# Linear attention and a balanced expert layer on one core: the attention half written out in an order set by a list scheduler, with k split on GpSimd

## The chip, the cores and the metric

The kernel runs on one core of a Trainium2 chip. A core has a matrix engine (TensorE, PE in the profile), VectorE (DVE), ScalarE (ACT), GpSimd (POOL) and a queue engine (SyncE, SP), which run their own instruction lists in order and wait for each other through semaphores. 16 DMA engines move data; SyncE issues to one DMA queue (q1) and GpSimd to another (q0). The metric is device time in microseconds (us).

## The reference

Two layers, one after the other. The first is linear attention with decay, for 4 batches x 8 heads x 768 positions x 64, in blocks of 64:

```
intra = (q_b k_b^T * Dmask) v_b            # Dmask = lam^(i-j) for i >= j
inter = (q_b * lam^(i+1)) kv_state
out_b = intra + inter
kv_state = lam^64 * kv_state + (k_b * lam^(63-i))^T v_b
```

Its output, 3072 tokens of 512, is x. The second layer gives each token to one of 8 experts: all 3072 x 8 logits `x @ w_gate` are walked from the largest down, a token goes to the expert of its first entry that still has room, and an expert has room for 384 tokens. Then each expert computes `relu(x w1) w2` on its tokens. Inputs and the output are float32.

## The kernel before

The attention is done in 24 chunks of 128 tokens and all 8 heads (6 chunks a batch). For one chunk, with names and lines of `before.py`:

- **loads**: q, k and v, 256 KB each, from SyncE (`load`, L949 to L953), buffers for four chunks (`aio`, bufs=4);
- **prep** (L956 on): k is rounded to fp16 on ScalarE (L960), and what is left of it is taken on VectorE (L961), both into a tile `kp` that interleaves the halves; v is scaled on GpSimd (`vs`, L963), rounded on ScalarE (`vh`, L966), and the remainder taken on GpSimd (`vl`, L968);
- **turns**: q and k are transposed on TensorE, and copied out by ScalarE and VectorE (`qh`, `ql`, `kT`);
- **scores** (L1005): three products a head into `S`; rounded on ScalarE (L1010), remainder on VectorE (L1011), masked on GpSimd (two `affine_select` a chunk, L1014, "masks" below);
- **inter, intra** (L1033, L1045) add up in `XL`; VectorE scales that into `xs` (L1050), SyncE stores it to `x_dram` (L1078);
- **state** (L1064): k^T v is added up in PSUM and read out as `sth`, `stl`;
- **gate**: x is transposed, split (`xh`, `xl` L1087), multiplied by `w_gate`, and the logits are copied out (L1103).

Chunks are numbered 0 to 23 below; "masks of chunk 20" are its two L1014 instructions. Each GpSimd, VectorE or ScalarE instruction named here works on 128 partitions x 512 elements.

`run` writes the stages of neighbouring chunks into a loop, and the Tile framework's own scheduler puts the instructions in order. Constants for the router (`constants`, among them an `iota` of 128 x 3072 on GpSimd, L42) are written in the loop's third step, and so are the first steps of the routing (`ranges`, `ranks`: largest logits, their ranks as threshold indicators `ind1`) near its end. Seven of the sixteen expert weight loads (`load_w`, L558, 1 MB each as they land in bf16, issued by GpSimd) are tied to logits of late chunks by a one-element copy (L557); two more (`range(7, 9)`) are tied to nothing, and the scheduler issued them early.

After the last logits the routing goes on by itself: counts on TensorE against indicators, `settle` on VectorE (L215, "the first settle"), further rounds, and then the first gather of tokens (L576) for the experts. From there on the experts run; the other seven weight loads, the gathers and the scatters of results (L626) all go through GpSimd's queue.

Of the kernel before, what the change touches and what calls it, by code (L numbers as in the profile page):

```python
# [23 lines left out]
class _Router:  # L24
# [11 lines left out]
    def constants(self):  # L36
        nc, rc, P = self.nc, self.rc, 128
        V, G = nc.vector, nc.gpsimd

        def iota(name, shape, pattern, base, mult=0, dt=BF16):  # L40
            a = rc.tile(shape, dt, name=name)
            G.iota(a, pattern=pattern, base=base, channel_multiplier=mult,  # L42
                   allow_small_or_imprecise_dtypes=True)
            return a

        self.i_kt = iota("i_kt", [P, P, 24], [[1, P], [0, 24]], 1)
        self.i_j = iota("i_j", [P, 29, 24], [[1, 29], [0, 24]], 0)
        self.i_t = iota("i_t", [P, 24, 24], [[0, 24], [128, 24]], 0)
        self.i_p = iota("i_p", [P, 1], [[0, 1]], 0, 1, F32)
        self.i_e = iota("i_e", [P, 8], [[1, 8]], 0, 0, F32)  # L50
        self.i_e1 = iota("i_e1", [P, 8], [[1, 8]], 1, 0, F32)
        self.i_et = iota("i_et", [P, 24, 8], [[0, 24], [1, 8]], -8)
        self.i_g8 = iota("i_g8", [P, 9, 24], [[1, 9], [0, 24]], -8)
        self.gbase = iota("gbase", [1, 9, 24], [[384, 9], [0, 24]], 1, 0, F32)
        i_k = self.i_kt[:, :, 0]
        kvec = []
        for m, sc in enumerate((16384, 128, 1, 4096)):
            kx = rc.tile([P, P], BF16, name=f"kvec{m}")
            V.tensor_scalar(kx, i_k, float(sc), None, OP.mult)
            kvec.append(kx)  # L60
        self.kvec = kvec
        ones = {}
        for sc in (16384, 128, 64, 1):
            o = rc.tile([P, P], BF16, name=f"ones{sc}")
            V.memset(o, float(sc))
            ones[sc] = o
        self.ones = ones
        ones3 = rc.tile([3, P], F32, name="ones3")
        V.memset(ones3, 1.0)
        self.ones3 = ones3  # L70
# [5 lines left out]
        sltm = rc.tile([P, P], BF16, name="sltm")  # L76
        V.tensor_scalar(sltm, slt, 1.0, None, OP.subtract)
        self.sltm = sltm
# [3 lines left out]
        self.rmask = rmask  # L82
        rmask5 = rc.tile([P, 8, 5], F32, name="rmask5")
# [13 lines left out]
        self.ind2 = rc.tile([P, P, 24], BF16, name="ind2")  # L97
        G.memset(self.ind2[:, 64:128, :], 0.0)

    def ranges(self, L, n, ps, tag, part):  # L100
# [3 lines left out]
        if part == 0:  # L104
            self.v0 = v0 = rc.tile([P, n], F32, name="v0")
            V.reduce_max(v0, L[:, 0:n, :], axis=AX.X)
            self.mn = mn = rc.tile([P, 2], F32, name="mn")
            V.tensor_reduce(mn[:, 1:2], L[:, 0:n, :].rearrange("p t e -> p (t e)"), axis=AX.X,
                            op=OP.min)
            self.mm = mm = rc.tile([P, 3], F32, name="mm")  # L110
            V.reduce_max(mm[:, 0:1], v0, axis=AX.X)
            V.tensor_reduce(mn[:, 0:1], v0, axis=AX.X, op=OP.min)
            V.tensor_scalar(mm[:, 1:3], mn, -1.0, None, OP.mult)
            return
        if part == 1:
# [618 lines left out]
def _exact_path(ctx, tc, L, router, moe, dram):  # L734
# [398 lines left out]
def kernel(  # L1133
# [12 lines left out]
    P = 128  # L1146
# [63 lines left out]
```

## Time and profile before

| | us |
|---|---|
| median of three runs | 319.54 (315.22 to 323.77) |
| the profiled execution | 321.75 |
| its span, first to last instruction | 320.0 |
| last logits copied (L1103) | 167.90 |
| first settle (L215) | 171.06 |
| first gather issued (L576) | 189.37 |

The span falls into the attention, to 168 us, the routing, to 189 us and in part to 206 us, and the experts. A row of the timeline gives the start and the length of an instruction; `x2` means two merged into one row.

### The profile page before, as it was taken

What the parts mean: (1) busy time and instruction counts of PE and PEld (TensorE: products, weight loads), DVE (VectorE), ACT (ScalarE), POOL (GpSimd) and SP (SyncE); (2) the same over time, 40 slices, a digit from 0 to 9 for tenths busy, and PEclk for the clock granted to TensorE, in tenths of its full rate; (3) what the DMA queues carried; (4) which work ended last, traced back from release to release, by engine and by line L of the source; (5) the groups of instructions that cost most, each with busy time, mean ns of one, the idle gap of its engine ahead of it and who ended that gap; (6) DMA issues with size and microseconds to landing.
All of it is one profiled execution on the core that took longest, in us unless ns stands there. A gap on an engine that the chain in (4) does not pass through costs nothing.

```text
span 320.0 us, 8964 instructions
## 1 busy us (share of the span) xinstructions
PE 257.0 (80%) x3621; PEld 202.1 (63%) x3621; DVE 187.2 (58%) x595; ACT 166.7 (52%) x297; POOL 163.5 (51%) x189
## 2 busy tenths in 40 slices
PE   1795979979898898883759987999766999899980
PEld 0674868867777787772647676666444666577750
DVE  4558688968987788746975654577717671000000
ACT  3757687878887788625220000454242455566650
POOL 5987466674757566733436024864254226435221
PEclk9999799999999999985767785799979999999997
DMA  8999999978989899999799308999999216244211
GB/s 144 218 178 201 242 228 241 203 169 193 201 187 198 183 200 190 198 205 203 134 180 222 59 5 108 162 188 204 238 228 256 97 58 107 99 96 103 73 69 38
DMA packets 96977, 52.05 MB, mean 163 GB/s; under 512 B 76961, under 2 KB 88225, under 8 KB 96929
## 3 DMA queue, kind: packets, MB, share of 16 engines
q0 software_dynamic: 17920, 26.22, 44.2%
q1 hardware_dynamic: 79008, 25.19, 36.9%
q8 instruction: 30, 0.49, 0.6%
q14 instruction: 19, 0.15, 0.1%
HBM read 58.74 MB, written 12.58 MB: 223 GB/s over the span
## 4 chain that ended last, share of the span: by engine, by line
PE 28%; DVE 21%; DMA 19%; issue 12%; ACT 9%; POOL 8%; SPq 0%; POOLq 0%; DVEq 0%; ACTq 0%
DMA out_dram<-oe,perm 11%; DMA kf<-in_k_dram 7%; PE p L607 5%; PE p L620 5%; DVE sp L1011 5%; DVE xs L1050 4%; ACT sp L1010 3%; PE XL L1101 3%; PE spare L193 3%; DVE ql L994 3%; PE S L1005 2%; DVE xl L1087 2%; DMA xe<-x_dram,perm 2%; POOL vs L963 2%; POOL sp L1014 2%
## 5 line engine op out<-in xcount | busy, mean ns | idle before, releaser
L607 PE MATMUL p<-xeT,w 128*128 128x256 bf16 (+1 forms) x512 | 50.2, 253 | 8.5 <-ACT hT L612 4.2
L607 PEld LDWEIGHTS <-w 128*128 128x128 bf16 x512 | 40.6, 100 | 17.1 <-issue 9.9
L1014 POOL TENSOR_SCALAR_AFFINE_SELECT sp<-sp 128x512 f32<-128x512 f32 x48 | 31.4, 663 | 33.7 <-DVE sp L1011 31.2
L626 POOL DMA_INDIRECT out_dram<-oe,perm x24 | 24.2, 1007 | 43.2 <-ACT oe L625 34.0
L620 PE MATMUL p<-w,hT 128*128 128x512 bf16 x192 | 45.8, 378 | 0.0
L576 POOL DMA_INDIRECT xe<-x_dram,perm x24 | 25.3, 1053 | 36.4 <-DVE B L306 15.0
L1010 ACT CAST sp<-S 128x512 bf16<-128x512 f32 x48 | 32.4, 743 | 19.1 <-PE S L1005 19.0
L612 ACT ACTIVATE hT<-p 128x512 bf16<-128x512 f32 (+1 forms) x64 | 31.0, 493 | 18.7 <-PE p L607 12.1
L1011 DVE TENSOR_TENSOR sp<-S,sp 128x512 bf16<-128x512 f32 x48 | 32.9, 732 | 6.5 <-ACT sp L1010 6.4
L963 POOL TENSOR_TENSOR vs<-vf,lamneg 128x512 f32<-128x512 f32 x24 | 27.3, 1139 | 9.9 <-DMA vf<-in_v_dram 6.2
L625 ACT COPY oe<-p 128x512 f32<-128x512 f32 x24 | 14.0, 587 | 34.2 <-PE p L620 20.4
L594 ACT COPY xeT<-pt 128x1024 bf16<-128x1024 bf16 (+1 forms) x16 | 12.8, 800 | 35.8 <-PE pt L590 34.2
L968 POOL TENSOR_TENSOR vl<-vs,vh 128x512 bf16<-128x512 f32 x24 | 28.4, 1183 | 5.7 <-ACT vh L966 5.4
L1005 PE MATMUL S<-qh,kT 64*128 64x128 f16 x384 | 28.8, 229 | 1.3 <-DVE sp L1011 1.3
L1045 PE MATMUL XL<-vh,sp 128*128 128x64 bf16 x384 | 25.7, 202 | 4.8 <-POOL sp L1014 4.2
L620 PEld LDWEIGHTS <-hT 128*128 128x128 bf16 x192 | 17.1, 97 | 17.8 <-issue 1.4
L1045 PEld LDWEIGHTS <-sp 128*128 128x128 bf16 x576 | 22.5, 104 | 8.4 <-POOL sp L1014 7.4
L977 PE MATMUL kT_ps<-identf,kp 128*128 128x128 f32 x96 | 17.6, 313 | 10.4 <-DVE mb L126 6.0
L961 DVE TENSOR_TENSOR kp<-kf,kp 128x512 f16<-128x512 f32 x24 | 20.0, 835 | 8.3 <-ACT kp L960 8.2
L960 ACT CAST kp<-kf 128x512 f16<-128x512 f32 x24 | 18.9, 789 | 10.8 <-DMA kf<-in_k_dram 10.8
L1005 PEld LDWEIGHTS <-kT 64*128 64x128 f16 x576 | 19.7, 99 | 6.5 <-issue 3.8
L1045 PE MATMUL XL<-vl,sp 128*128 128x64 bf16 x192 | 23.1, 201 | 0.0
(259 smaller groups left out, 584.8 us busy)
## 6 DMA issues: line engine op xcount, KB each, us to landing
w<-in_moe_w_dram POOLq DMA_DIRECT2D x16, 1024.0 KB
qf<-in_q_dram SPq DMA_DIRECT2D x24, 256.0 KB, 4.7
kf<-in_k_dram SPq DMA_DIRECT2D x24, 256.0 KB, 5.2
vf<-in_v_dram SPq DMA_DIRECT2D x24, 256.0 KB, 5.3
x_dram<-xs SPq DMA_DIRECT2D x24, 256.0 KB, 3.8
xe<-x_dram,perm POOLq DMA_INDIRECT x24
out_dram<-oe,perm POOLq DMA_INDIRECT x24
lam_sb<-in_lam_dram SPq DMA_DIRECT2D x1, 4.0 KB, 2.5
```

Of the source, the lines that this page charges most:

```text
L576: nc.gpsimd.indirect_dma_start(out=xe[:, c, :], out_offset=None, in_=self.x_dram, in_offset=bass.IndirectOffsetOnAxis(ap=pm, axis=0), boun ...
L607: nc.tensor.matmul(p1[:, f, 0:n, :], self.w1t[e][:, kc, fc * P : (fc + 1) * P], j["xeT"][:, kc, 0:n, :], start=(kc == 0), stop=(kc == 3), ...
L612: nc.scalar.activation(hT[:, fp, :, 0:n, :], p1[:, :, 0:n, :], ACT.Relu)
L620: nc.tensor.matmul(p2, j["hT"][:, kc // 2, kc % 2, c, :], self.w2t[e][:, kc, :], start=(kc == 0), stop=(kc == 7))
L626: ins = nc.gpsimd.indirect_dma_start(out=self.out, out_offset=bass.IndirectOffsetOnAxis(ap=j["perms"][c], axis=0), in_=oe, in_offset=None, ...
L963: nc.gpsimd.tensor_tensor(vs, vf, self.lamneg[:, t, :, None].to_broadcast([P, 8, 64]), OP.mult)
L968: nc.gpsimd.tensor_tensor(vl, vs, vh, OP.subtract)
L1005: nc.tensor.matmul(S[a][:, hp, :], kT[r, hp, :, ks], qq[r, hp, :], start=(i == 0), stop=(i == 2))
L1010: nc.scalar.copy(s[:, :, :, 1], S[a])
L1011: nc.vector.tensor_tensor(s[:, :, :, 0], S[a], s[:, :, :, 1], OP.subtract)
L1014: nc.gpsimd.affine_select(out=sf, in_=sf, compare_op=OP.is_ge, fill=0.0, base=0, pattern=[[0, 4], [1, P]], channel_multiplier=-1)
L1045: nc.tensor.matmul(X[a][:, hp, :], sp[a][:, hp, :, ss], vv[:, h, :], start=(first and hp == 0 and i == 0), stop=(i == 2), skip_group_check ...
```

## The change

The attention is rewritten as small functions, one for each instruction group, and `OPS` lists them with the engine, an assumed duration and what each waits for (`ldk` of chunk g after `state` and `Tk` of chunk g-7, and so on). `_Plan.emit` is a list scheduler: it runs these through assumed engine times, takes the ready operation of lowest `OFF[name] + g * 4.6` on each engine, and so writes the program order of all five engines, which the framework then keeps (`manual_schedule`). In the parts:

- **k**: no fp16 rounding on ScalarE and no `kp` tile. The upper 16 bits of each float32 are read as bf16 in place; the rest is taken by one subtraction into the lower 16 bits, in place, on GpSimd (`kp0`, L1099). The planner's table gives `kp0` of even chunks to VectorE and of odd ones to GpSimd; the function always issues it on GpSimd.
- **loads** go up to six chunks ahead (k: seven buffers), and `xs` has seven buffers.
- **PSUM**: the transposes of q, k and x have a bank each (`QT`, `KT`, `XT`); the logits are added up in the bank of `XT`.
- **router**: its constants are spread over the chunks (`pool_constants`, `dve_constants`), the large `iota` in four pieces; `ranges` and `ranks` yield after each instruction, and are planned as operations of their own.
- **weights**: nine loads (`lw`) are planned on GpSimd, the first after the last load of v, each after the one before and after masks of chunks 15 to 23.

The routing after its first steps, the experts and the order of their loads are as before.

```diff
-        kp = self.wk.tile([P, 8, 64, 2], F16, tag="kp", bufs=4)
-        nc.scalar.copy(kp[:, :, :, 1], kf)
-        nc.vector.tensor_tensor(kp[:, :, :, 0], kf, kp[:, :, :, 1], OP.subtract)
...
+    def kp0(self, g):
+        kf = self.kpair(self.d[g])
+        lo = kf.bitcast(F16).rearrange("p (c j s) -> p c j s", c=4, s=2)[:, :, :, 0]
+        self.nc.gpsimd.tensor_tensor(lo, kf.rearrange("p (c j) -> p c j", c=4), self.ksplit(kf)[0],
+                                     OP.subtract)
...
+    def ksplit(self, f):
+        hi = f.bitcast(BF16).rearrange("p (c j s) -> p c j s", c=4, s=2)[:, :, :, 1]
+        lo = f.bitcast(F16).rearrange("p (c j s) -> p c j s", c=4, s=2)[:, :, :, 0]
+        return hi, lo
...
-        self.io = ctx.enter_context(tc.tile_pool(name="aio", bufs=4))
+        self.io = ctx.enter_context(tc.tile_pool(name="aio", bufs=6))
...
+    OPS = (
+        ("ldq", "SP", 1.10, None, "Tq-6"),
+        ("ldk", "SP", 1.10, None, "state-7 Tk-7"),
...
+        ("kp0", None, 0.78, None, "ldk"),
...
+        ("mk1", "Pool", 0.66, None, "spl1"),
...
+                if name == "kp0" and eng is None:
+                    eng, dur = (("DVE", 0.78), ("Pool", 1.17))[g % 2]
...
+                    m = min(max(free[e], est[i]) for i in a)
+                    i = min((ops[i][6], i) for i in a if max(free[e], est[i]) <= m + 0.05)[1]
...
-            if s == 2:
-                router.constants()
-            if 19 <= s <= 21:
-                router.ranges(logits, 18, attn.pt, "T", s - 19)
-            if s == 22:
-                router.ranks(logits, 0, 10)
...
-            if 18 <= s <= 24:
-                moe.load_w(s - 18, logits[0:1, s - 2, 0:1])
...
+        for m in range(9):
+            plan.op("lw", m, "Pool", 0.9, lambda m=m: moe.load_w(m),
+                    [("ldv", 23), ("mk1", min(15 + m, 23)), ("lw", m - 1)], 0, 4.6)
...
-    for m in range(7, 9):
-        moe.load_w(m)
```

How it moves instructions is shown at two places. The first is GpSimd around the weight loads. In its list of before, the first weight load that is tied to logits (`w_0_78`) stands ahead of the masks of chunk 18 (`sp_2955` and `sp_2959`):

```order
L968 TENSOR_TENSOR vl<-vs,vh 128x512
L558 DMA w_0_78<-in_moe_w_dram 128x4x1024
L1014 AFFINE_SELECT sp_2955<-sp_2955 128x512
L1014 AFFINE_SELECT sp_2959<-sp_2959 128x512
L963 TENSOR_TENSOR vs<-vf,lamneg 128x512
L1014 AFFINE_SELECT sp_3088<-sp_3088 128x512
L968 TENSOR_TENSOR vl<-vs,vh 128x512
L1014 AFFINE_SELECT sp_3092<-sp_3092 128x512
```

The changed list around its first weight load (`kf<-kf` is `kp0`; L1113 is `vs`, L1124 `vl`, L1184 a mask; `sp_2809` and `sp_2840` are the masks of chunk 18, the `kf` row ahead of the load is `kp0` of chunk 22):

```order
L1113 TENSOR_TENSOR vs<-vf,lamneg 128x512
L1124 TENSOR_TENSOR vl<-vs,vh 128x512
L1184 AFFINE_SELECT sp_2705<-sp_2705 128x512
L1099 TENSOR_TENSOR kf<-kf 128x512
L638 DMA w_0_70<-in_moe_w_dram 128x4x1024
L1184 AFFINE_SELECT sp_2809<-sp_2809 128x512
L1184 AFFINE_SELECT sp_2840<-sp_2840 128x512
L1124 TENSOR_TENSOR vl<-vs,vh 128x512
L1113 TENSOR_TENSOR vs<-vf,lamneg 128x512
L1184 AFFINE_SELECT sp_2942<-sp_2942 128x512
L1099 TENSOR_TENSOR kf<-kf 128x512
L1113 TENSOR_TENSOR vs<-vf,lamneg 128x512
```

The first weight load now stands behind `kp0` of chunk 22 with only one more `kp0` and two more `vs` to come, and each chunk has one GpSimd instruction more, `kp0`, which runs four to five chunks ahead of the masks. Up to the second mask of chunk 20 the changed list holds, from the second mask of chunk 0 on, 21 `kp0`, 22 `vs`, 22 `vl`, 40 masks, `identb`, the four pieces of the large `iota` and two weight loads.

The second place is VectorE around the last logits. Before, the copy of the last logits (`logits<-Lo`) is followed by six rows of `ranks` for the last 128 tokens, and then by the first settle (`S<-cps`):

```order
L156 TENSOR_TENSOR ind_607<-q_3814,i_kt 128x128x3
L168 TENSOR_SCALAR r_q_603<-y_3819 128x3
L1103 COPY logits<-Lo 128x8
L143 TENSOR_REDUCE r_v<-logits 128x1
L145 TENSOR_SCALAR y_3906<-r_v,lo,sc 128x1
L146 TENSOR_SCALAR y_3906<-y_3906 128x1
L147 TENSOR_SCALAR r_zv<-y_3906 128x1
L149 TENSOR_SCALAR ind_608<-kvec_568,r_zv 128x128
L150 TENSOR_TENSOR r_ohb<-logits,r_v 128x8
L215 TENSOR_SCALAR S<-cps 128x8
```

In the changed list the last logits' copy (the L1247 row) stands in the midst of `ranks` of the first ten chunks:

```order
L1235 TENSOR_TENSOR xl<-XT,xh 128x512
L231 TENSOR_TENSOR r_ohb<-logits,r_v 128x80
L241 TENSOR_SCALAR y_3748<-r_zv 128x10
L243 TENSOR_SCALAR r_q_3524<-y_3748 128x10
L1247 COPY logits<-XT 128x8
L246 TENSOR_TENSOR ae_3752<-r_ohb,i_et 128x80
L207 TENSOR_REDUCE r_v<-logits 128x1
L248 TENSOR_REDUCE r_am_3526<-ae_3752 128x10
L207 TENSOR_REDUCE r_v<-logits 128x10
```

From the last `xs` to that copy there are 22 rows, and from the copy to the first settle 32 more, among them `ranks` of chunks 10 to 19 and of 20 to 22 whole.

## Rows read from the trace of the kernel before

**Rows 1.** The page: its first line.

```profile
span 320.0 us, 8964 instructions
```

**Rows 2.** Windows: stretch, length, busy us of each engine (instructions), granted clock, DMA, GB/s.

```profile
43.00:120.00 77.00, 66.64 (x1417) 57.82 (x1418) 63.81 (x113) 60.74 (x110) 48.51 (x56) 1.00 0.90 200
147.00:170.00 23.00, 15.05 (x257) 12.76 (x258) 19.88 (x68) 7.94 (x14) 10.83 (x14) 0.65 0.93 171
206.00:247.00 41.00, 32.88 (x293) 21.86 (x291) 26.45 (x156) 16.31 (x26) 19.50 (x20) 0.96 1.15 217
```

**Rows 3.** Groups of instructions, 43 to 120 us: busy us, mean ns, idle before.

```profile
L1014 POOL TENSOR_SCALAR_AFFINE_SELECT sp<-sp 128x512 f32<-128x512 f32 x28 | 18.0, 651 | 26.7 <-DVE sp L1011 26.7
L968 POOL TENSOR_TENSOR vl<-vs,vh 128x512 bf16<-128x512 f32 x14 | 16.3, 1164 | 1.0 <-ACT vh L966 0.7
L963 POOL TENSOR_TENSOR vs<-vf,lamneg 128x512 f32<-128x512 f32 x14 | 15.5, 1107 | 1.2 <-DMA vf<-in_v_dram 1.2
L960 ACT CAST kp<-kf 128x512 f16<-128x512 f32 x15 | 11.9, 796 | 0.0
L961 DVE TENSOR_TENSOR kp<-kf,kp 128x512 f16<-128x512 f32 x14 | 11.5, 818 | 0.0
```

**Rows 4.** The chain of waits, whole span: start us, length us, what.

```profile
2.25 4.07 DMA kf<-in_k_dram
...
129.28 16.78 DMA kf<-in_k_dram
...
228.64 17.41 DMA out_dram<-oe,perm
```

**Rows 5.** Timeline of GpSimd: start us, length us, instruction, idle before.

```profile
1.82 3.33 POOL L42 IOTA i_kt<- 128x3072 bf16 x1
...
17.86 1.23 POOL L1014 TENSOR_SCALAR_AFFINE_SELECT sp<-sp 128x512 f32<-128x512 f32 x2
...
21.71 0.84 POOL L558 DMA_DIRECT2D w<-in_moe_w_dram  x1
...
67.68 1.48 POOL L963 TENSOR_TENSOR vs<-vf,lamneg 128x512 f32<-128x512 f32 x1
...
122.12 0.81 POOL L558 DMA_DIRECT2D w<-in_moe_w_dram  x1 [1.74 <-DVE w L557]
...
135.61 1.22 POOL L1014 TENSOR_SCALAR_AFFINE_SELECT sp<-sp 128x512 f32<-128x512 f32 x2
...
161.59 1.23 POOL L1014 TENSOR_SCALAR_AFFINE_SELECT sp<-sp 128x512 f32<-128x512 f32 x2 [2.40 <-DVE sp L1011]
...
189.37 1.59 POOL L576 DMA_INDIRECT xe<-x_dram,perm  x1 [15.02 <-DVE B L306]
```

**Rows 6.** DMA queues, 110 to 150 us: packets, MB, share of 16 engines.

```profile
q1 hardware_dynamic: 13469, 4.72, 51.0%
q0 software_dynamic: 2123, 3.17, 49.1%
```

**Rows 7.** Timeline of VectorE.

```profile
163.74 0.69 DVE L1050 TENSOR_TENSOR xs<-XL,lampow 128x512 f32<-128x512 f32 x1 [1.05 <-PE XL L1045]
...
167.90 0.22 DVE L1103 COPY logits<-Lo 128x8 f32<-128x8 f32 x1
...
171.06 0.17 DVE L215 TENSOR_SCALAR S<-cps 128x8 bf16<-128x8 f32 x1 [1.52 <-PE cps L241]
```

**Rows 8.** Groups of VectorE's instructions, 147 to 170 us.

```profile
L1011 DVE TENSOR_TENSOR sp<-S,sp 128x512 bf16<-128x512 f32 x6 | 4.1, 718 | 0.3 <-ACT sp L1010 0.3
L1087 DVE TENSOR_TENSOR xl<-xT_ps,xh 128x512 bf16<-128x512 f32 x4 | 2.7, 684 | 0.2
L156 DVE TENSOR_TENSOR ind<-q,i_kt 128x1280 bf16<-128x1280 bf16 (+1 forms) x3 | 2.4, 800 | 0.0
L1050 DVE TENSOR_TENSOR xs<-XL,lampow 128x512 f32<-128x512 f32 x3 | 2.1, 688 | 1.3 <-PE XL L1045 1.3
...
L1103 DVE COPY logits<-XL 128x8 f32<-128x8 f32 x3 | 0.5, 159 | 0.5 <-PE XL L1101 0.5
```

More of the change, by code (lines that the diff above doesn't have):

```diff
@@ L238, in first @@
             nc.tensor.matmul(cps, self.ind1[:, :, t], ohb[:, t, :], start=(t == 0), stop=False)
-        self.ranks(L, 23, 24)
+        for _ in self.ranks(L, 23, 24):
+            pass
         self.warm(0.6)
@@ L242, in first @@
         _, nm1 = settle(cps, self.ones[64])
-        self.more(23, 24)
+        for _ in self.more(23, 24):
+            pass
         z2 = sp.tile([P, 24], BF16, name="z2")
@@ new lines, in intra @@
+    def intra(self, g, a):
+        d = self.d[g]
+        first = g % 6 == 0
+        if "XL" not in d:
+            d["XL"] = self.p1.tile([128, 2, 8, 64], F32, tag="X", name="XL")
+        for hp in range(4):
+            for i, (ss, vv) in enumerate(((1, d["vh"]), (1, d["vl"]), (0, d["vh"]))):
+                self.nc.tensor.matmul(d["XL"][:, a, hp, :], d["sp"][a][:, hp, :, ss],
+                                      vv[:, 2 * hp + a, :],
+                                      start=(first and hp == 0 and i == 0), stop=(i == 2),
+                                      skip_group_check=True)
@@ L1052, in intra, with store, turn_x, xh @@
         d["xs"] = xs
[L1054 to L1057 removed]
+    def store(self, g):
+        self.nc.sync.dma_start(out=self.x_dram[g * 128 : (g + 1) * 128, :],
+                               in_=self.d[g]["xs"].rearrange("p c a d -> p (c a d)"))
+    def turn_x(self, g):
+        d = self.d[g]
+        d["xT_ps"] = self.turn(lambda hp: d["xs"][:, hp].rearrange("p a d -> p (a d)"), "XT")
+    def xh(self, g):
+        d = self.d[g]
+        d["xh"] = self.wk.tile([128, 4, 128], BF16, tag="xh", name="xh")
+        self.nc.scalar.copy(d["xh"], d["xT_ps"])
@@ new lines, in xl, with gate @@
+    def xl(self, g):
+        d = self.d[g]
+        d["xl"] = self.wk.tile([128, 4, 128], BF16, tag="xl", name="xl")
+        self.nc.vector.tensor_tensor(d["xl"], d["xT_ps"], d["xh"], OP.subtract)
+    def gate(self, g):
+        d = self.d[g]
+        d["Lp"] = Lp = d["xT_ps"][:, 0, 0:8]
+        for hp in range(4):
+            for i, (xx, ww) in enumerate(((d["xh"], self.wgh), (d["xh"], self.wgl),
+                                          (d["xl"], self.wgh))):
+                self.nc.tensor.matmul(Lp, xx[:, hp, :], ww[:, hp, :], start=(hp == 0 and i == 0),
+                                      stop=(hp == 3 and i == 2), skip_group_check=True)
```

511 lines of the change are left out of this document (306 added, 205 removed), and 24 rows, old and new, of the table OPS.

## The prediction

> **What bounds the kernel now.** I read the windows first, then the groups of instructions in the steady stretch, then the chain of waits, then the timelines of GpSimd and VectorE. The profiled span is 320.0 us [rows 1]; the run around it took 321.75, 1.75 more, and lies 0.7% above the median of the runs shown, 319.54.
>
> The steady stretch, 43 to 120 us, holds 14 chunks (14 `vs`), 5.50 us each [rows 2, 3]. TensorE is busy 66.64 us there (4.76 a chunk, 87%), VectorE 63.81 (83%), ScalarE 60.74 (79%), GpSimd 48.51 (63%), and the DMA engines 0.90 [rows 2]. No engine is full: the reader is to see four of them that pass each chunk round. GpSimd's masks waited 26.7 us for VectorE [rows 3].
>
> The ends of the attention are worse than its middle. The second mask of chunk 0 ends at 19.09 us (17.86 + 1.23), that of chunk 20 at 136.83, that of chunk 23 at 162.82 [rows 5]: 5.89 us a chunk up to 20, and 8.66 for the last three. The chain shows why: 16.78 us from 129.28, in which a load of k is under way, where the first took 4.07 [rows 4]. At that time the weight loads, from 122.12 on [rows 5], share the DMA engines with the attention's loads almost evenly, 49.1% to 51.0% [rows 6]. An early weight load at 21.71 and the large `iota` of 3.33 us [rows 5] lie in the start.
>
> After the last logits (167.90) the first settle comes at 171.06 [rows 7], and the first gather at 189.37 [rows 5]. The experts then wait for scatters behind weight loads until 246 (17.41 us from 228.64 [rows 4], DMA share 1.15 [rows 2]).
>
> **The change, part by part**, by the marks where GpSimd ends its masks.
>
> *Start.* GpSimd's constants and the two early weight loads go away from here. Up to the second mask of chunk 0 the new list has three `kp0`, two `vs`, one `vl` and two masks. `kp0` is not in the trace. From below it is the same subtraction on VectorE, 0.818 us [rows 3]; from above the slowest `vs`, 1.48 us [rows 5]. I take `vl`, 1.164 us [rows 3]: the same engine, also a subtraction of a bf16 operand from a float32 one with a 16-bit result. With 1.107 for `vs` and 0.651 for a mask [rows 3] that is 8.2 us from the landing of k at 6.32 [rows 4], so 14.5; some wait for the first rounding makes it 15.0, against 19.09: **4.1 us less**.
>
> *Chunks 0 to 20.* ScalarE loses the rounding of k (0.796) and VectorE its remainder (0.818) [rows 3]; GpSimd gains `kp0`. Per chunk GpSimd goes from 3.47 us to about 4.6, VectorE falls from 4.56 to 3.7, ScalarE from 4.34 to 3.5, and TensorE keeps its 4.76: GpSimd and TensorE are now the ones to watch. As `kp0`, `vs` and `vl` run ahead, GpSimd must do 21, 22 and 22 of them for 40 masks in this piece: 24.4 + 24.4 + 25.6 + 26.0, with `iota` 3.3, `identb` 0.5 and two weight issues of 0.84 [rows 5], 106.0 us. Durations overlap a little: the three groups sum to 49.8 where the window has 48.51 [rows 2, 3], so 103.2. How full can it run? The fullest engine of the steady stretch stood at 87%; the limit is 100%; I take the middle, 93%. 103.2 / 0.93 = 111.0 us, 5.55 a chunk, against 117.7 now: **6.7 less**. So I expect no better pace than the steady one of now: the gain is that the start no longer falls behind it. It puts the end of chunk 20's masks at 126.0.
>
> *DMA.* The chunk's 1.05 MB (four times 256 KB, in MB of 10^6 bytes) at this pace is 189 GB/s, less than the 200 of the steady stretch and the 217 of a full one [rows 2], and the loads are five to six chunks ahead; I cost them at nothing. Stores of `xs` stand between loads on SyncE: a load behind such a store is late by what chunk g is late, but has four chunks, 22 us, before it is used.
>
> *Weights.* The first goes out behind `kp0` of chunk 22, two `vs` short of the end, so the stall of 16.78 us has nobody left to hit; what comes last then is TensorE. The last three chunks need 3 x 4.76 = 14.3 us, since GpSimd has little but masks left, against 25.99 now: **11.7 less**. The cover on the other side: four weights leave after the masks of chunk 20 or later. At 217 GB/s [rows 2] a weight's 1.05 MB takes 4.8 us, so the last, issued near 143, lands at 162, ten before the gather, below.
>
> *First steps of the routing.* From the masks of chunk 23 to the end of its `xs` it is 1.6 us (162.82 to 164.43 [rows 5, 7]), and stays so. From there to the first settle it is 6.6 us now [rows 7]. In the new list VectorE has 54 rows there: most of `ranks`, which it now did in the gaps of the stall. Their price: VectorE is busy 19.88 us from 147 to 170 [rows 2]; off go the splits 4.1, `xl` 2.7, `xs` 2.1, logits 0.5 [rows 8] and three rows of a remainder's size (0.7 each as `xl`'s mean), which leaves about 8. Two `xl` (1.4) and two constants (0.8 each, as the indicator's 800 ns [rows 8]) come to it: 11. The settle then waits for the last counts, 1.5 us as now [rows 7]: 12.5 in all, **5.9 more**.
>
> *The rest*, from the first settle on, has the same instructions in the same order: 148.9 us. The granted clock was 0.65 from 147 to 170 [rows 2], that is, partly at 1.2 GHz, after TensorE had stood idle in the stall. Without it the routing may start at 2.4; I cost it at nothing and count it to the low end.
>
> Sum: 4.1 + 6.7 + 11.7 - 5.9 = 16.6 us; 321.75 - 16.6 = 305.1 for a run like the profiled one, and at the median, 0.7% less, **303 us**. The first settle then lies near 154.4, the first gather near 172.7.
>
> **Two rules beside the rows.** For TensorE's share the row says 87% [rows 2]. The Trainium skill, Perfetto Trace Analysis, section Identifying the Most-Contended Engine, says that busy time of matmuls is not a good measure and that of weight loads is: here 57.82 of 77 us, 75%. By it the last three chunks would need 12.4 us and the sum would be 1.9 lower. On `kp0` the rows say that a subtraction takes 1.164 us on GpSimd and 0.818 on VectorE, 1.42 times [rows 3]; the rule that speaks against this edit stands under the second rival.
>
> **The rivals** (times at the median).
>
> 1. *GpSimd runs full.* Its prep work is four to five chunks ahead of its masks, so something is mostly ready; against it, it never passed 63% in the steady stretch [rows 2]. 103.2 us instead of 111.0: 295. Chance 0.15.
>
> 2. *`kp0` costs more and GpSimd bounds.* Its operands are every second 16-bit word, which no GpSimd row of before shows. At twice VectorE's row, 1.64 us, the piece to chunk 20 is 10.5 us longer: 313. Chance 0.10. This is what the Trainium skill, GPSIMD Engine Reference, section Engine selection, gives: work on elements with two inputs belongs on VectorE, and is about twice as slow on GpSimd.
>
> 3. *The weights don't stand behind the loads in fact.* Their place rests on the planner's times. If the last loads are late by then, a wait like the 16.78 returns, 12.7 above the first load's 4.07 [rows 4]: 315 to 316. Against it: some 20 us of GpSimd work lie between the `vs` that frees the last buffer of v and the first weight. Chance 0.07.
>
> 4. *Slower: prep ahead of masks in one queue.* The planner gave half of the `kp0` to VectorE; on GpSimd they all stand in line with the masks, and that line was balanced for less. Where one `kp0` and one `vs` a chunk hold a mask up, the pace is 5.55 + 1.164 + 1.107 = 7.8 us and chunk 20 ends 45 us later: 348. It decides for slower by 2% from a pace of 6.7 us on. For it: the masks were waited for, and waited, in the steady stretch [rows 3]; against it, prep is taken four chunks ahead, and TensorE has masked chunks to go on with. Chance 0.06.
>
> **Numbers.** Forecast 0.62, rivals 0.15, 0.10, 0.07, 0.06. Bounds: `kp0` at 0.818 or 1.48 us moves the sum by -7.6 or +7.0; GpSimd at 100% or 87% by -7.8 or +8.2; the last two pieces by some 3 each way. Together about 12 each way, 291 to 315, which holds the forecast, most of the first rival, and the second; the third lies at its edge. A change under 2% (313.1 to 325.9) can hardly be told here: the three runs spread over 2.7%. Faster by more: forecast, the first rival and a little of the rest, 0.79; within 2%: 0.14; slower: 0.07.
>
> **What would show it.** Second masks of chunks 0, 20 and 23 near 15, 126 and 140; `kp0` near 1.16 us; GpSimd above 85% busy between; no k load over 10 us late in the attention; first settle 12 to 13 us after the last `xs`; and 149 us from there to the end. Wrong would be a chunk pace over 6, `kp0` over 1.5, or a gather that waits for weights.

## The result, and the profile after

The changed kernel took 297.96 us (four runs, 297.33 to 300.45), the kernel before beside it 319.12 (315.22 to 323.77): ratio 0.939, 95% interval 0.928 to 0.950. The ratio is that of the means of all runs within 1.5% of the fastest of their kernel, so it differs a little from that of the two medians. The forecast was 303 us, in a range of 291 to 315. The profiled run took 298.12; its page begins:

```profile
span 296.3 us, 8922 instructions
```

By the marks of the prediction:

| | before | predicted | after |
|---|---|---|---|
| second mask of chunk 0 ends | 19.09 | 15.0 | 16.69 |
| from there to chunk 20 | 117.7 | 111.0 | 100.4 |
| chunks 21 to 23 | 26.0 | 14.3 | 11.9 |
| last mask to end of the last `xs` | 1.6 | 1.6 | 2.6 |
| last `xs` to first settle | 6.6 | 12.5 | 14.9 |
| first settle to the end of the span | 148.9 | 148.9 | 149.8 |

They come from GpSimd's timeline of the changed kernel (start us, length us, instruction, idle before):

```profile
16.05 0.64 POOL L1184 TENSOR_SCALAR_AFFINE_SELECT sp<-sp 128x512 f32<-128x512 f32 x1 [0.78 <-DVE sp L1179]
...
105.33 1.00 POOL L638 DMA_DIRECT2D w<-in_moe_w_dram  x1
...
115.83 1.22 POOL L1184 TENSOR_SCALAR_AFFINE_SELECT sp<-sp 128x512 f32<-128x512 f32 x2
...
127.65 1.26 POOL L1184 TENSOR_SCALAR_AFFINE_SELECT sp<-sp 128x512 f32<-128x512 f32 x2
...
163.31 1.60 POOL L656 DMA_INDIRECT xe<-x_dram,perm  x1 [19.06 <-DVE B L386]
```

and from VectorE's:

```profile
130.86 0.69 DVE L1215 TENSOR_TENSOR xs<-XL,lampow 128x512 f32<-128x512 f32 x1 [0.30 <-PE XL L1206]
...
137.92 0.17 DVE L1247 COPY logits<-XT 128x8 f32<-128x8 f32 x1
...
146.47 0.17 DVE L293 TENSOR_SCALAR S<-cps 128x8 bf16<-128x8 f32 x1 [1.08 <-PE cps L320]
```

These answer to [rows 5, 7]: 5.02 us a chunk to chunk 20 (100.4 / 20) where it was 5.89, and the first gather at 163.31 where it was 189.37. The windows (columns as in [rows 2]; the DMA column adds up the packets' times and comes out above 1 in several rows) of the steady stretch, of the last three chunks, and of the last `xs` to the first settle:

```profile
43.00:110.00 67.00, 60.70 (x1352) 54.87 (x1351) 53.54 (x97) 52.77 (x96) 64.75 (x77) 0.97 1.03 228
...
117.05:128.90 11.85, 10.30 (x267) 9.14 (x265) 11.14 (x31) 7.55 (x13) 11.74 (x23) 1.00 1.13 211
...
131.55:146.47 14.92, 6.29 (x63) 5.21 (x64) 11.92 (x55) 1.17 (x2) 6.08 (x9) 0.50 1.18 224
```

GpSimd is busy 64.75 of 67 us (97%; 63% in [rows 2]), the DMA share is 1.03 at 228 GB/s (0.90 at 200), TensorE is at 91%. In the last three chunks GpSimd is busy 11.74 of 11.85 us, TensorE 10.30. In the third window VectorE is busy 11.92 of 14.92 us. GpSimd's groups from 43 to 110 us, against [rows 3]:

```profile
L1184 POOL TENSOR_SCALAR_AFFINE_SELECT sp<-sp 128x512 f32<-128x512 f32 x28 | 17.5, 640 | 0.0
L1124 POOL TENSOR_TENSOR vl<-vs,vh 128x512 bf16<-128x512 f32 x15 | 17.4, 1168 | 0.0
L1113 POOL TENSOR_TENSOR vs<-vf,lamneg 128x512 f32<-128x512 f32 x15 | 15.7, 1047 | 1.0 <-DMA vf<-in_v_dram 1.0
L1099 POOL TENSOR_TENSOR kf<-kf 128x512 f16<-128x512 f32 x13 | 13.5, 1048 | 1.2 <-DMA kf<-in_k_dram 1.0
```

GpSimd, which stood idle for 26.7 us before masks, stands idle before them no more; `kp0` takes 1.048 us. SyncE issues the last loads here (timeline):

```profile
98.57 1.10 SPq L1093 DMA_DIRECT2D kf<-in_k_dram  x1
99.76 1.05 SPq L1093 DMA_DIRECT2D qf<-in_q_dram  x1
100.90 1.91 SPq L1220 DMA_DIRECT2D x_dram<-xs  x1
102.90 0.39 SPq L1093 DMA_DIRECT2D vf<-in_v_dram  x1
```

The last k leaves at 98.57, ahead of the first weight at 105.33. In the kernel before, a load of k left at 129.28 [rows 4], behind the weight of 122.12 [rows 5].

So the forecast had direction and range right, and one large term wrong by 10.7 us: the piece to chunk 20. That the sum came within 5 us is in part luck: this piece and the last three chunks were shorter than forecast by 13 us together, and the other four rows of the table longer by 6. The runs below ask where the 17.4 us of the piece to chunk 20 came from.

### The profile page after: what moved, and what is told of

Its sections match the earlier page's. It is cut to its first block, busy times and chain, and to the rows that moved or that the text cites. A ratio compares the mean times of both kernels' runs of the same rounds, so it can differ in the third digit from the quotient of the medians.

```text
span 296.3 us, 8922 instructions
## 1 busy us (share of the span) xinstructions
PE 240.6 (81%) x3608; PEld 193.8 (65%) x3621; DVE 168.3 (57%) x564; ACT 151.6 (51%) x273; POOL 182.2 (61%) x216
## 4 chain that ended last, share of the span: by engine, by line
PE 33%; POOL 21%; DMA 19%; issue 10%; DVE 10%; ACT 4%; SPq 0%; POOLq 0%; ACTq 0%; DVEq 0%
DMA out_dram<-oe,perm 12%; PE p L687 8%; PE p L700 5%; POOL kf L1099 5%; POOL vl L1124 5%; POOL sp L1184 4%; POOL vs L1113 4%; DMA vf<-in_v_dram 4%; DMA kf<-in_k_dram 3%; PE spare L271 3%; PE S L1166 2%; PE KT L1129 2%; POOL out_dram L706 2%; PE psC L396 1%; DVE sp L1179 1%
## 5 line engine op out<-in xcount | busy, mean ns | idle before, releaser
L700 PE MATMUL p<-w,hT 128*128 128x512 bf16 x179 | 43.8, 379 | 1.0 <-issue 0.2
L1179 DVE TENSOR_TENSOR sp<-S,sp 128x512 bf16<-128x512 f32 x48 | 34.6, 745 | 9.1 <-ACT sp L1173 8.9
L705 ACT COPY oe<-p 128x512 f32<-128x512 f32 x24 | 14.1, 586 | 39.6 <-PE p L700 25.0
L1184 POOL TENSOR_SCALAR_AFFINE_SELECT sp<-sp 128x512 f32<-128x512 f32 x48 | 30.1, 640 | 1.8 <-DVE sp L1179 1.7
L1129 PE MATMUL KT<-identf,kf 128*128 128x128 f32 x96 | 16.3, 295 | 15.9 <-POOL kf L1099 15.8
L1099 POOL TENSOR_TENSOR kf<-kf 128x512 f16<-128x512 f32 x24 | 25.0, 1047 | 6.5 <-DMA kf<-in_k_dram 6.3
L1124 POOL TENSOR_TENSOR vl<-vs,vh 128x512 bf16<-128x512 f32 x24 | 27.9, 1169 | 0.6 <-ACT vh L1119 0.5
L1113 POOL TENSOR_TENSOR vs<-vf,lamneg 128x512 f32<-128x512 f32 x24 | 25.1, 1047 | 1.4 <-DMA vf<-in_v_dram 1.4
L1206 PE MATMUL XL<-vh,sp 128*128 128x64 bf16 x384 | 23.4, 196 | 0.5 <-POOL sp L1184 0.4
L1166 PE MATMUL S<-qh,kT 64*128 64x128 f16 x384 | 21.6, 221 | 1.3 <-ACT qh L1151 0.7
L1129 PEld LDWEIGHTS KT<-identf,kf 128*128 128x128 f32 x96 | 10.9, 148 | 17.5 <-POOL kf L1099 17.5
L1206 PE MATMUL XL<-vl,sp 128*128 128x64 bf16 x192 | 21.1, 196 | 0.2 <-issue 0.2
L1166 PEld LDWEIGHTS <-kT 64*128 64x128 bf16 (+1 forms) x576 | 17.0, 96 | 5.6 <-issue 3.3
```

Source lines behind the costliest of these rows:

```text
L700: nc.tensor.matmul(p2, j["hT"][:, kc // 2, kc % 2, c, :], self.w2t[e][:, kc, :], start=(kc == 0), stop=(kc == 7))
L1099: self.nc.gpsimd.tensor_tensor(lo, kf.rearrange("p (c j) -> p c j", c=4), self.ksplit(kf)[0], OP.subtract)
L1113: self.nc.gpsimd.tensor_tensor(d["vs"], d["v"], self.lamneg[:, g % 6, :, None].to_broadcast([128, 8, 64]), OP.mult)
L1124: self.nc.gpsimd.tensor_tensor(d["vl"], d["vs"], d["vh"], OP.subtract)
L1129: self.nc.tensor.transpose(ps[:, hp, :], src(hp), self.identf)
L1166: self.nc.tensor.matmul(S[a][:, hp, :], kk[r, hp, :], qq[r, hp, :], start=(i == 0), stop=(i == 2))
```

## The experiments

Times are medians, beside the 297.96 us of the changed kernel; "pace" is from the second mask of chunk 0 to that of chunk 20, divided by 20. The first two ask what bounds the changed kernel.

**Half of `kp0` on VectorE.**

```diff
-        self.nc.gpsimd.tensor_tensor(lo, ...
+        eng = (self.nc.vector, self.nc.gpsimd)[g % 2]
+        eng.tensor_tensor(lo, ...
```

> The changed kernel with the k remainder of even chunks on VectorE and of odd chunks on GpSimd; all orders unchanged. Theory G (GpSimd sets the pace: it is busy 64.75 of 67 us from 43 to 110 in the changed kernel): 0.52 us a chunk leave GpSimd, the pace falls from 5.02 to 4.6 or 4.7 us, and the second mask of chunk 20 ends at 109 to 111 in place of 117; time 290 to 293. Theory D (the DMA engines set it: share 1.03, 223 to 228 GB/s in the same stretch): the pace stays at 5.0 and the time at 297 to 299, with GpSimd's share falling to 87%. Third possibility: VectorE (80% there) becomes late with the remainders that the masks wait for; pace above 5.1, time 300 or more.

298.67 us (298.31 to 299.14), pace 5.11. GpSimd falls to 60.0 of 67 us and nothing is gained: GpSimd now waits for loads of k, 8.5 us, as theory D has it, and theory G alone falls. The third possibility, VectorE late for the masks, is not what the rows show: GpSimd stood idle for no mask (0.0), and from chunk 5 to 20 the pace is that of the changed kernel (4.89 and 4.87 us). Window 43 to 110 us, then three groups of it:

```profile
43.00:110.00 67.00, 57.19 (x1280) 50.63 (x1277) 54.83 (x93) 48.88 (x88) 60.02 (x70) 0.97 1.00 229
```

```profile
L1185 POOL TENSOR_SCALAR_AFFINE_SELECT sp<-sp 128x512 f32<-128x512 f32 x27 | 17.2, 654 | 0.0
...
L1100 POOL TENSOR_TENSOR kf<-kf 128x512 f16<-128x512 f32 x8 | 8.4, 1054 | 8.5 <-DMA kf<-in_k_dram 8.5
...
L1100 DVE TENSOR_TENSOR kf<-kf 128x512 f16<-128x512 f32 x6 | 6.1, 1025 | 0.0
```

The same instruction took 1.025 us on VectorE and 1.054 on GpSimd.

**Half of the q loads.**

```diff
+        if n == "q" and g % 2:
+            self.d[g][n] = self.d[g - 1][n]
+            return
```

> The changed kernel with q of odd chunks not loaded (they compute on the q of the chunk before), so that part of the output is another; every instruction of the compute engines stays. Traffic of a chunk falls from 1.05 to 0.92 MB on average. Theory G (GpSimd sets the pace): the pace to chunk 20 stays at 5.0 us, GB/s falls by an eighth, time 296 to 298. Theory D (DMA sets it): the pace falls by up to 0.6 us a chunk, time 286 to 291.

294.96 us (293.92 to 296.95), pace 4.88, between the two theories. Same window:

```profile
43.00:110.00 67.00, 60.48 (x1383) 54.36 (x1382) 54.23 (x98) 52.35 (x95) 66.91 (x79) 1.00 0.83 189
```

With the DMA engines relieved (0.83), GpSimd is busy 66.91 of 67 us. Two limits lie within some 3% of each other: relieving GpSimd runs into the transfers, relieving the transfers into GpSimd.

**Weights where they were before.**

```diff
-        for m in range(9): ... [("ldv", 23), ("mk1", min(15 + m, 23)), ("lw", m - 1)]
+        for m in (7, 8): ... [("mk1", 0)] ...
+        for m in range(7): ... [("lg", 16 + m)] ...
```

> The changed kernel with the weight loads where the kernel before has them: two after the masks of chunk 0, seven tied to logits of chunks 16 to 22, each a place in the same list. Theory W (weight loads beside the last loads are what cost the last three chunks 26 us before): a load of k or q is over 10 us late again near 125, the last three chunks take 20 to 25 us in place of 11.9, time 306 to 310. Rival P (loads six chunks ahead and a full GpSimd cover the sharing of the DMA engines): last three chunks at 12 to 15 us, time 297 to 301.

311.59 us (311.20 to 311.81). The size is that of theory W, the place is not: the last three chunks take 11.7 us, as in the changed kernel, and chunks 0 to 5 take 38.9 in place of 27.3. GpSimd's timeline shows why:

```profile
17.71 1.13 POOL L638 DMA_DIRECT2D w<-in_moe_w_dram  x1
...
24.56 0.83 POOL L638 DMA_DIRECT2D w<-in_moe_w_dram  x1
29.36 1.04 POOL L1099 TENSOR_TENSOR kf<-kf 128x512 f16<-128x512 f32 x1 [3.96 <-DMA kf<-in_k_dram]
...
37.68 1.04 POOL L1099 TENSOR_TENSOR kf<-kf 128x512 f16<-128x512 f32 x1 [4.58 <-DMA kf<-in_k_dram]
```

Two weights beside the first loads cost 11.6 us. The other seven, which go out from 119.92 on, cost the last three chunks nothing: in this list the last load (of v) has left at 110.79. From chunk 5 to 20 the pace is 4.89 us (4.87 in the changed kernel, 5.63 before).

**The same nine weights in mid-attention**, behind the masks of chunks 8 to 16.

```diff
-                    [("ldv", 23), ("mk1", min(15 + m, 23)), ("lw", m - 1)], 0, 4.6)
+                    [("mk1", 8 + m), ("lw", m - 1)], 0, 4.6)
```

> The changed kernel with its nine weight loads after the masks of chunks 8 to 16 in place of behind the last load of v: they go out from about 58 us on, in the midst of the loads for the attention. In the run with the weights placed as before, two of them beside the first loads cost 11.5 us by chunk 5, and seven that fell behind the last load cost nothing. Theory W (a weight beside the loads costs what it takes of full DMA engines, 4.8 us each): the four to seven that get in before the last load cost 20 to 35 us, the last load of k is issued at 120 or later in place of 98.6; time 318 to 333. Rival P (in mid-attention the loads are six chunks ahead, which covers it; the start was special): under 10 us, time 298 to 308.

337.58 us (336.40 to 338.78): theory W, and beyond its upper end. Eight weights go out ahead of the last load of v, which leaves at 143.06, and the last `xs` ends at 169.69 in place of 131.55: 38.1 / 8 = 4.8 us a weight, what 1.05 MB take at 217 GB/s [rows 2]. The waits from 55 to 150 us (what waits for what: us in all, times, longest):

```profile
POOL kf L1099 <- DMA kf<-in_k_dram: 33.0, 6, 11.6
```

Six chunks of loads ahead don't cover it: with the DMA engines at their limit, a weight pushes every later load back by its own length.

**The kernel before, with its weights late**, all nine tied to logits of chunks 19 to 22.

```diff
-            if 18 <= s <= 24:
-                moe.load_w(s - 18, logits[0:1, s - 2, 0:1])
+            for m in {21: (0, 1), 22: (2, 3), 23: (4, 5), 24: (6, 7, 8)}.get(s, ()):
+                moe.load_w(m, logits[0:1, s - 2, 0:1])
-    for m in range(7, 9):
-        moe.load_w(m)
```

> The kernel before with all nine weight loads after its last loads (tied to logits of chunks 19 to 22 by the one-element copy, none early); nothing else. Theory W (the 16.78 us wait for k is the weights' doing): the wait goes, the last three chunks fall from 26 us to 15 to 17, less what the routing's first steps give back; time 309 to 313 and the start 1 to 2 us earlier. Rival P (the last chunks are slow for lack of loads ahead, or for the order of the work): under 3 us from the change, time 316 to 320.

331.24 us (329.01 to 333.64): slower, which neither theory said. The wait of 16.78 us is gone (the last load of v leaves at 142.56, the first weight at 156.55), and the last three chunks fall from 26.0 to 19.9 us. But the framework's scheduler, given other ties, puts all engines' work into another order, and the pace rises from 5.89 to 6.62 us:

```profile
43.00:110.00 67.00, 53.80 (x1000) 45.50 (x1001) 48.60 (x84) 45.38 (x80) 38.11 (x41) 0.92 0.72 159
```

No engine is over 81% and the DMA share is 0.72. To chunk 20 the computation is the same, and no weight goes out, where before four did; what else differs is the order, and over 20 chunks the run loses 14.6 us. As a test of the weights it is spoilt by that; it pointed to order as the suspect.

**Loads four chunks ahead** in the written list, as far as before.

```diff
-        ("ldq", "SP", 1.10, None, "Tq-6"),
-        ("ldk", "SP", 1.10, None, "state-7 Tk-7"),
+        ("ldq", "SP", 1.10, None, "Tq-4"),
+        ("ldk", "SP", 1.10, None, "state-5 Tk-5"),
...
-        ("ldv", "SP", 1.10, None, "vs-6"),
+        ("ldv", "SP", 1.10, None, "vs-4"),
```

> The changed kernel with the loads four chunks ahead (k: five buffers, q and v four), as the kernel before has them, and planned so. Theory L (what raised the pace from 5.89 to 5.02 us a chunk is that loads run far ahead and keep the DMA engines full): the DMA share from 43 to 110 us falls from 1.03 to 0.95 or less, GpSimd and VectorE wait for k and v, the pace is 5.4 us or more and the time 306 to 315. Rival O (the order of the work and k split in place raised it, four chunks are enough): pace 5.0 to 5.1, time 297 to 300.

299.94 us (299.27 to 301.57), pace 5.13, DMA share 1.02. Rival O, by the time: the deeper loads are worth some 2 us, and not surely that, since the runs of the two kernels overlap.

**k as before, in the written list**: rounded on ScalarE, the remainder on VectorE, in tiles of its own.

```diff
-        self.nc.gpsimd.tensor_tensor(lo, kf..., self.ksplit(kf)[0], OP.subtract)
+        self.nc.vector.tensor_tensor(lo, self.d[g]["k"]..., self.ksplit(kf)[0], OP.subtract)
+    def khi(self, g):
+        d["kp"] = self.wk.tile([128, 8, 64, 2], F16, tag="kp", name="kp", bufs=4)
+        self.nc.scalar.copy(d["kp"][:, :, :, 1], d["k"])
...
-        ("ldk", "SP", 1.10, None, "state-7 Tk-7"),
+        ("ldk", "SP", 1.10, None, "kp0-5"),
...
-                    [("ldv", 23), ("mk1", min(15 + m, 23)), ("lw", m - 1)], 0, 4.6)
+                    [("vs", 23), ("mk1", min(15 + m, 23)), ("lw", m - 1)], 0, 4.6)
```

> The changed kernel's list with k split as in the kernel before: a rounding to fp16 on ScalarE and the remainder on VectorE, both into a tile of its own (k loads up to five chunks ahead, since these tiles take room); the weights planned behind vs of chunk 23, so that they can't pass the loads. All the rest is planned by the same rules. ScalarE then has some 95% of work in the stretch from 43 to 110 us and VectorE 96%, at the changed kernel's pace. Theory S (the split in place on GpSimd, with the engines that it relieves, is what the pace of 5.02 us comes from): 5.5 us or more a chunk to chunk 20, time 307 to 318. Rival O (the written-out order is what counts, in the loads and in the rows of every engine; the split only shifts work): 5.0 to 5.25 us a chunk, time 297 to 304.

295.99 us (294.96 to 296.61), pace 4.84: not slower than the split on GpSimd. The 2 us by which the run is faster are not the attention's: its last `xs` ends at 132.18, 0.6 us later than the changed kernel's, and its first settle comes at 147.92, 1.5 us later. What follows, 149.8 us there, took 146.6 here (146.6 to 150.5 in all the runs). The window, then three groups of 43 to 110 us:

```profile
43.00:110.00 67.00, 63.02 (x1439) 55.95 (x1436) 64.59 (x111) 62.16 (x112) 54.79 (x63) 1.00 0.97 225
```

```profile
L1189 POOL TENSOR_SCALAR_AFFINE_SELECT sp<-sp 128x512 f32<-128x512 f32 x29 | 19.8, 692 | 7.0 <-DVE sp L1184 6.0 <-PE KT L1134 0.5 <-DVE logits L1252 0.3
L1118 POOL TENSOR_TENSOR vs<-vf,lamneg 128x512 f32<-128x512 f32 x15 | 17.4, 1162 | 0.6
...
L1099 DVE TENSOR_TENSOR kp<-kf,kp 128x512 f16<-128x512 f32 x14 | 13.7, 976 | 0.0
```

VectorE runs at 96%, ScalarE at 93%, TensorE at 94%. The same work, on the same engines as before, now passes in 4.84 us a chunk, and the attention ends within 0.6 us of where it ends with the split on GpSimd: theory S falls.

**k's remainder all on VectorE, in place**, and planned so.

```diff
-        self.nc.gpsimd.tensor_tensor(lo, ...
+        self.nc.vector.tensor_tensor(lo, ...
...
-                    eng, dur = (("DVE", 0.78), ("Pool", 1.17))[g % 2]
+                    eng, dur = ("DVE", 0.82)
```

> The changed kernel with the k remainder of every chunk on VectorE, and planned so: GpSimd falls from 97 to some 76% of the stretch from 43 to 110 us, VectorE rises from 80 to some 96% (13 instructions of about 0.82 us). Theory D (the DMA engines set the pace, GpSimd just keeps up): 5.0 to 5.1 us a chunk, time 297 to 301. Theory V (VectorE can't run so full, since its instructions stand in a chain with ScalarE and TensorE): pace 5.2 to 5.5, time 302 to 309. It also gives the price of the same instruction on VectorE, 0.7 to 0.82 us expected against 1.047 on GpSimd.

310.67 us (306.30 to 313.42; the profiled run 311.73), for another reason than either theory's. To chunk 16 the pace is 4.99, near theory D's. Then, in the chain of waits:

```profile
105.61 0.32 SPq L1093
105.93 0.05 issue
105.98 19.96 DMA kf<-in_k_dram
125.96 0.74 DVE kf L1099
```

The planner put the first weight at 96.52, ahead of the last k at 105.98, and that load took 19.96 us. This is the prediction's third rival, in a neighbour of the changed kernel: the place of the weights rests on planned times. The instruction asked for took 0.894 us on VectorE, more than the 0.7 to 0.82 expected:

```profile
L1099 DVE TENSOR_TENSOR kf<-kf 128x512 f16<-128x512 f32 x13 | 11.6, 894 | 0.0
```

The last four runs ask about the first steps of the routing, 14.9 us from the last `xs` to the first settle.

**Planned sooner**, and the constants on GpSimd (and the first of those on VectorE) with it.

```diff
-            plan.op("pc", ... [("pc", i - 1), ("mk1", i // 2)], 1e6 + i)
+            plan.op("pc", ... [("pc", i - 1), ("mk1", i // 2)], 60.0 + 6 * i)
...
-             ("lg", 18), None),
+             ("lg", 17), None),
...
-             ("lg", 20), ("Tx", 21)),
+             ("lg", 18), ("Tx", 19)),
...
-             ... ("lg", 21), ("Tx", 22)),
+             ... ("lg", 19), ("Tx", 20)),
...
```

> The changed kernel with the first steps of the routing planned three chunks sooner where the data allow it (ranges over 18 chunks still) and its constants on GpSimd sooner; VectorE has 44 rows in place of 55 from the last xs to the first settle. Theory R (VectorE's rows there set the settle: it is busy 11.9 of the 14.9 us): 14.9 falls to about 12, time 294 to 296. Rival (the settle waits for the counts on TensorE at the lower clock, 0.50 there): 14 to 15 stays, time 297 to 299.

298.19 us (297.57 to 301.17). The settle comes 11.1 us after the last `xs`, as theory R has it, but that itself ends 4.6 us later, at 136.15: nothing gained. One of the moved rows, in VectorE's timeline, and what GpSimd did then:

```profile
118.33 3.25 DVE L168 TENSOR_SCALAR mm<-mn 128x2 f32<-128x2 f32 x1
```

```profile
118.60 0.63 POOL L1186 TENSOR_SCALAR_AFFINE_SELECT sp<-sp 128x512 f32<-128x512 f32 x1
119.17 1.38 POOL L71 MEMSET ind<- 128x1536 bf16 x1
120.52 1.04 POOL L1115 TENSOR_TENSOR vs<-vf,lamneg 128x512 f32<-128x512 f32 x1
121.68 0.64 POOL L1186 TENSOR_SCALAR_AFFINE_SELECT sp<-sp 128x512 f32<-128x512 f32 x1
```

An instruction on two elements a partition lasts 3.25 us and ends as GpSimd leaves a gap (121.56 to 121.68).

**Ranges over 14 chunks**, so that most of the ranks come ahead of the last logits.

```diff
-            plan.op("pc", ... [("pc", i - 1), ("mk1", i // 2)], 1e6 + i)
+            plan.op("pc", ... [("pc", i - 1), ("mk1", i)], 30.0 + 4 * i)
...
-            (self.ranges(L, 18, attn.p1, "XT", 0), ... ("lg", 18), None),
+            (self.ranges(L, 14, attn.p1, "XT", 0), ... ("lg", 13), None),
...
```

> As the run with the routing planned sooner, but the ranges are taken over the first 14 chunks in place of 18, so that nearly all of the ranks come before the last logits: VectorE has 22 rows from the last xs to the first settle in place of 55. Theory R: the settle comes 6.5 to 8 us after the last xs in place of 14.9, and VectorE, 80% busy before, takes the rows in its gaps; time 289 to 293. Rival: the rows delay the masks and xs of the last chunks by as much as they save, xs of chunk 23 at 136 or later; time 295 to 299.

306.62 us (305.14 to 313.42). The settle comes 6.0 us after the last `xs`, as theory R has it, but that ends at 147.60, 16 us later, as its rival has it and worse: GpSimd's constants, moved sooner too, lengthen its full stretch (chunks 0 to 5 take 31.8 us in place of 27.3, with 3.7 us of `iota` in them), and chunks 17 to 20, among whose work the ranks now stand, take 26.7 in place of 20.2, with VectorE busy 25.1 of them. Three small rows on VectorE take 2.2 to 3.1 us.

**One small row more per chunk on VectorE.**

```diff
+        if 4 <= g < 12:
+            self.nc.vector.tensor_scalar(ex, self.lampow[:, 0, :], 2.0, None, OP.mult)
+        elif 12 <= g < 20:
+            self.nc.vector.reduce_max(ey, self.lampow[:, 0, :], axis=AX.X)
```

> The changed kernel with one small VectorE instruction more per chunk behind ql: for chunks 4 to 11 a tensor_scalar of 128x8 from one on-chip tile to another, for chunks 12 to 19 a maximum over the same 128x8; nothing reads their results. Theory K (while GpSimd runs without gaps, a tensor_scalar between on-chip tiles has to wait until it pauses, as the three of 2.2 to 3.3 us in the runs with the routing planned sooner suggest; a maximum does not): the eight tensor_scalar take 0.6 to 3 us each in the mean, the maxima 0.15 to 0.2; the piece to chunk 12 is 3 to 12 us later, time 300 to 309. Rival (those three waited for something of their own): all sixteen take 0.1 to 0.2 us, time 297 to 300.

298.46 us (296.00 to 299.75). VectorE's groups, 20 to 120 us:

```profile
L1159 DVE TENSOR_SCALAR ex<-lampow 128x8 f32<-128x8 f32 x8 | 5.2, 644 | 0.0
...
L1162 DVE TENSOR_REDUCE ey<-lampow 128x1 f32<-128x8 f32 x8 | 1.2, 149 | 0.0
```

Same size, the one in the first part of a stretch in which GpSimd is 97% busy, the other in the second: 0.644 us (0.34 to 0.97) and 0.149. Theory K holds at its lower end in the rows, its rival in the time: the piece to chunk 12 is 1.2 us longer, not 3 to 12, since VectorE, at 82% there, has room for the 5.2 us.

**Less ahead of the settle**: the four rows of each part that nothing needs before it are done once behind it, and 22 chunks are ranked in one part.

```diff
-        for a, b in ((0, 10), (10, 20), (20, 23)):
+        for a, b in ((0, 22), (22, 23)):
...
-        yield from self.more(a, b)
...
-        for _ in self.more(23, 24):
+        for _ in self.more(0, 24):
```

> The changed kernel with less of the ranks ahead of the first settle: the four rows of each part that nothing needs before it are done once, for all 24 chunks, behind it, and the first 22 chunks are ranked in one part in place of two and a bit; VectorE has 33 rows in place of 55 from the last xs to the first settle, and nothing moves into the stretch in which GpSimd is full. Theory R (VectorE's rows set the settle): it comes 9.5 to 11.5 us after the last xs in place of 14.9, time 293 to 295. Rival (the rows taken away come back behind the settle, or the counts at TensorE's lower clock set it): 297 to 299.

293.12 us (six runs, 292.73 to 294.47; 0.925 of before, 0.920 to 0.931), the fastest kernel here; its runs and those of the changed kernel don't overlap.

```profile
130.63 0.69 DVE L1214 TENSOR_TENSOR xs<-XL,lampow 128x512 f32<-128x512 f32 x1 [0.37 <-PE XL L1205]
...
140.96 0.17 DVE L292 TENSOR_SCALAR S<-cps 128x8 bf16<-128x8 f32 x1 [1.39 <-POOL Z L260]
```

The settle comes 9.6 us after the last `xs`, and from there to the end it is 150.2 us, about as in the changed kernel: what is saved stays saved. The granted clock rose too, from 0.50 to 0.65 between the two marks, so the rival with TensorE's clock needs a look elsewhere. In the run with half of `kp0` on VectorE the clock there was 0.64, and with as many rows as in the changed kernel the settle came after 14.5 us. So it is the rows and not the clock:

```profile
133.06:147.52 14.46, 5.71 (x63) 4.66 (x64) 11.82 (x56) 1.17 (x2) 6.07 (x9) 0.64 1.18 225
```

## Why the prediction was right, and where it was not

**Chunks 0 to 20** (6.7 us forecast, 17.4 measured): this step failed. It priced the piece by how full GpSimd can run, the middle of the fullest engine's 87% and 100%, and concluded "no better pace than the steady one of now". GpSimd ran at 97%, and `kp0` and `vs` took 1.05 us where 1.164 and 1.107 were taken, so the rows that it counted took 4 us less: rival 1's number came, and GpSimd did run full. But GpSimd is only one of two limits of the new kernel, and not what made the pace. With half of `kp0` gone from it the time stays, and with k as before, GpSimd at 82%, the pace is 4.84 us. The kernel before took 5.50 us a chunk for the same work on the same engines; the masks for which GpSimd waited 26.7 us [rows 3] were the sign that they could do better. Of the 17.4 us, 6.0 lie in chunks 0 to 5 (33.3 to 27.3 us), where the two early weights alone cost 11.6 when put back into the new list; the prediction named the weight at 21.71 [rows 5] but gave it no price. The other 11.3 lie in chunks 5 to 20 (84.4 to 73.1), and stay with the weights as before (73.4), with four loads ahead (74.7), and with k as before (70.1). What remains is the written-out order with the PSUM banks and buffers that go with it; these were not taken apart, and that the order is the larger part is argued, from the run of the kernel before in another order, and not shown.

**The DMA engines** were costed at nothing. That was too low a price for a resource at 1.03: an eighth less traffic is worth 3.0 us.

**Last three chunks** (11.7 forecast, 14.1 measured): half of the mechanism holds. The weights left behind the last load and no load was late. The price of a weight, 4.8 us, was right to a tenth in mid-attention (at the start two cost 5.8 each). But TensorE is not what came last, and 4.76 us a chunk was too much for it: it was busy 10.30 of 11.85 us, 3.4 a chunk. GpSimd, which was said to have "little but masks left", was busy 11.74: beside the masks stood 4.9 us of the router's constants and 2.5 of weight issues. So 14.3 us had the wrong reason, if on the safe side. TensorE's 87% [rows 2] was no ceiling either: from 43 to 110 us it stood at 91% in the changed kernel and at 94% with k as before. The Trainium skill, Perfetto Trace Analysis, section Identifying the Most-Contended Engine, names the weight loads' share as a better measure of the room that is left; that rose from 75% [rows 2] to 82%, and the traces agree that there was room.

**Start** (4.1 forecast, 2.4 measured): the rows took 7.7 us where 8.2 were forecast, but between them GpSimd waited 2.9 us where 0.5 was put: the masks of chunk 0 waited 0.96 and 0.78 us for VectorE, the rest went to loads and to `vh`.

**Last mask to last `xs`** was put at no change and took 1.0 us more.

**First steps of the routing** (5.9 more forecast, 8.3 measured): VectorE's rows set it, as said: 54 rows give 14.9 us, 43 give 11.1, 34 give 9.6 and 21 give 6.0. The 11 us of work were 11.9; the step left out the waits for ScalarE's `xh` (1.1 us) and between rows. The window's granted clock was 0.50, that is 1.2 GHz, so the hope for 2.4 GHz there fell.

**The rest** was put at no change and measured 0.9 us more. **Rivals:** `kp0` at 1.64 us did not come. On VectorE the same remainder took 0.818 [rows 3], 0.894, 0.976 and 1.025 us in four runs, so GpSimd's 1.048 is 1.02 to 1.28 times as long. About twice, as in the Trainium skill, GPSIMD Engine Reference, section Engine selection, is not what these rows show. Weights ahead of the loads did not come in this kernel, and came in its neighbour. Prep ahead of masks did hold masks up: from 43 to 110 us a mask started 2.0 us after its remainder was done on VectorE (0.2 before, means). It cost next to nothing, since TensorE waited for a mask once, and five times for a late `kp0` (who waits for whom: us in all, times, longest):

```profile
PE KT L1129 <- POOL kf L1099: 5.6, 5, 1.9
...
PEld L1206 <- POOL sp L1184: 0.6, 1, 0.6
```

## What to carry to other kernels

Four engines at 60 to 87% with waits all round were no floor here: ask what a better order of the same rows would reach before pricing what an edit takes off one engine. With the DMA engines near a share of 1, a background transfer cost its full length to all loads behind it, although they ran six chunks ahead; tie it to the last load itself, not to a planned time. Work that fills gaps late in a chain was best removed or put behind the point that waits; moving it into a full stretch gave back what it saved.

## What the runs showed of the hardware

- VectorE and GpSimd slow each other. With the subtraction of k, which reads two on-chip tiles, on VectorE (k as before, 43 to 110 us), a mask took 0.692 us, `vs` 1.162 and `vl` 1.227; with it on GpSimd 0.640, 1.047 and 1.168. Within that one run the masks that overlapped the subtraction took 0.88 us in the mean and the others 0.63; `vs` took 1.27 and 1.04. VectorE's subtraction took 0.73 to 0.76 us in the kernel before where nothing ran on GpSimd beside it, and 0.818 in the mean of all [rows 3]; with a fuller GpSimd the means are 0.894 to 1.025. The Trainium skill, SBUF — State Buffer, section Who interferes with whom, says that such an instruction contends with GpSimd's reads; the rows agree.
- A `tensor_scalar` of 128x8 between on-chip tiles took 0.644 us beside a full GpSimd, a maximum over the same (a `tensor_reduce`) 0.149. The same section says that the later of the two waits until the first has finished, and that a maximum never contends. The eight rows agree: none is longer than one GpSimd instruction of that stretch (`vl`, 1.168 us). The row of 3.25 us spans three GpSimd instructions; why it had to wait for a gap stays open.
